# Nine-token partitions, row-tiled attention and two early rounds of three experts in an attention-plus-experts kernel

## The chip, the cores and the metric

One core of one Trainium2 chip. The time is device microseconds (us) of one execution; a shorter time is better. The runs landed on several chips of the kind, and the kernel before does not take the same time on all of them: its medians were 599.9, 585.1, 599.4 and 585.0 us on the four chips of the experiments (called A, B, C and D here). So kernels are compared within one chip, through the kernel before that ran there too. Where times of two chips stand side by side, the text says so.

Engines in the profile: PE is TensorE (PEld its weight loads), DVE VectorE, ACT ScalarE, POOL GpSimd (it issues the cast loads and all gathers and scatters), SP SyncE (it issues the transposing reads).

## The reference

Linear attention with a feature map, whose result is the token matrix x, then a noisy top-2 router and eight experts.

```python
# q, k, v: (8 batches, 8 heads, 576 tokens, 64) float32
phi = lambda x: np.where(x > 0, x, np.exp(x) - 1.0) + 1.0
kv  = einsum('bhsd,bhse->bhde', phi(k), v);  z = phi(k).sum(axis=2)
x   = einsum('bhsd,bhde->bhse', phi(q), kv) / (phi(q).z + 1e-6)   # -> (4608, 512)
noisy = x @ w_gate + log1p(exp(x @ w_noise)) * noise              # (4608, 8)
# ... the two largest per token, softmax of the two -> top2, top2_w
for e in range(8):                       # w1 (512,1024), w2 (1024,512)
    h = maximum(x[mask_e] @ w1[e], 0);  out[mask_e] += top2_w * (h @ w2[e])
```

## The kernel before

It handles the eight batches in four groups of two. For each group: loads (with a cast to bf16), feature map, `kv`, `num`, routing, then a **dispatch**: 18 indirect transfers on POOL that write each token's row twice into `x_sorted`, sorted by expert. When all four groups are dispatched the experts run, 10 tiles of 128 rows each (80 tiles in all): a transposing read `xt`, `mm1` (first layer), `mm2` (second layer, called the tail of a tile), and per tile a **gather** of what the token's first expert wrote to `out` (into a tile `L`) and a **scatter** of the sum (from a tile `y`). A bank is one buffer of PSUM, where the matmul results stand until DVE or ACT takes them.

```python
main = lambda t, b: t[b, :, 0:512, :].rearrange("h (p c) d -> p h (c d)", c=4)   # + 64-token tails
...
for ci in range(NC):                                   # num: 9 blocks of tokens
    for hp in range(4):
        nc.tensor.matmul(out=ps[:, hp, 0:KVW], lhsT=pqs[j][:, hp, ...], rhs=kvbds[j][:, hp, :], ...)
    ...                                                # four DVE operations per block
# ---- (cut) experts
for e in range(E):
    gate, si, gi = self.meta(...)
    for n in (512, 512, 256):
        xt = ...; nc.sync.dma_start(out=xt, in_=self.x_sorted[...], transpose=True)
        hT = self.mm1(w1, xt, n)
        if prev is not None:
            flush(prev)                                # mm2, y, scatter of the block before
        if t0 == 0:
            if e + 3 < E: self.load_w(e + 3)
            for t in range(T_CAP):                     # all gathers of the expert at once
                L[t] = self.gather(gi[:, t : t + 1]) if e > 0 else None
        prev = ...
# pools: weights 3, xt 4, L 12, y 6; PSUM: 4 banks for h, 3 for y
```

A scheduler fixes each engine's order at build time; at run time an engine waits at the head of its list (n3_one below shows it on DVE: 14.75 us behind an operation of 0.17).

Of the kernel before, what the change touches and what calls it, by code (L numbers as in the profile page):

```python
# [15 lines left out]
P = 128  # L16
# [6 lines left out]
NG = 4  # L23
NC = 9
T_CAP = 10
CAP = T_CAP * P
REGION = N_TOK
ROW_W = HD + 16
BIG = 1.0e6
KVW = 162  # L30

# [6 lines left out]
def build_constants(ctx, tc, consts, w_gate, w_noise, noise):  # L38
    nc = tc.nc
    c = {}  # L40

# [19 lines left out]

    c8 = consts.tile([P, E], FP32, name="c8")
    nc.gpsimd.iota(c8[:], pattern=[[-1, E]], base=E, channel_multiplier=0,
                   allow_small_or_imprecise_dtypes=True)
    c["c8"] = c8

    tokid = consts.tile([P, NC], FP32, name="tokid")
    nc.gpsimd.iota(tokid[:, 0:8], pattern=[[S, 2], [1, 4]], base=0, channel_multiplier=4,
                   allow_small_or_imprecise_dtypes=True)
    for half in range(2):  # L70
        nc.gpsimd.iota(tokid[64 * half : 64 * half + 64, 8:9], pattern=[[0, 1]],
                       base=512 + S * half, channel_multiplier=1,
                       allow_small_or_imprecise_dtypes=True)
# [14 lines left out]

    wst = consts.tile([P, 4, 16], FP32, name="wst")
# [11 lines left out]

    noise_sb = consts.tile([P, NG, NC, E], FP32, name="noise_sb")
    for b in range(B):
        g, j = divmod(b, 2)
        nc.scalar.dma_start(
            out=noise_sb[:, g, 4 * j : 4 * j + 4, :],
            in_=noise[b * S : b * S + 512, :].rearrange("(p c) e -> p (c e)", c=4),
        )
    for j in range(2):
        src = noise[512 + j * S : 512 + j * S + 64, :]  # L110
        src = bass.AP(tensor=src.tensor, offset=src.offset,
                      ap=[src.ap[0], [2 * S * E, NG], [1, E]])
        nc.scalar.dma_start(out=noise_sb[64 * j : 64 * j + 64, :, 8, :], in_=src)
# [4 lines left out]
    c["carry"] = carry  # L118
    return c


class PhaseA:
    def __init__(self, ctx, tc, q, k, v, x_sorted, c):
        self.tc, self.nc, self.c = tc, tc.nc, c
        self.q, self.k, self.v, self.x_sorted = q, k, v, x_sorted
        nc = tc.nc
        pool = lambda name, bufs, **kw: ctx.enter_context(tc.tile_pool(name=name, bufs=bufs, **kw))
        self.ld = pool("A_ld", 3)
        self.mx = pool("A_mx", 2)
        self.pers = pool("A_pers", 1)  # L130
        self.tmp = pool("A_tmp", 2)
        self.php = pool("A_php", 2)
        self.kvp = pool("A_kvp", 3)
        self.pq = pool("A_pq", 3)
        self.rt = pool("A_rt", 2)
        self.ps_kv = pool("A_ps_kv", 2, space=PSUM)
        self.ps_t = pool("A_ps_t", 2, space=PSUM)
        self.ps_num = pool("A_ps_num", 2, space=PSUM)
        self.vt = []
        for i in range(4):  # L140
            t = self.pers.tile([P, 12, 256], BF16, name=f"v{i}")
            nc.vector.memset(t[:, 8:12, :], 1.0)
            self.vt.append(t)
        self.vm = []
        for i in range(2):
            t = self.pers.tile([P, 12, D], BF16, name=f"vm{i}")
            nc.vector.memset(t[:, 8:12, :], 1.0)
            self.vm.append(t)
        self.xrow = []
        for i in range(2):  # L150
            t = self.pers.tile([P, NC, ROW_W], BF16, name=f"xrow{i}")
            nc.vector.memset(t[:, :, HD:ROW_W], 0.0)
            self.xrow.append(t)

    def load(self, g):
        nc = self.nc
        st = {"g": g, "k": [], "q": [], "v": []}
        km = self.mx.tile([P, 8, D], BF16, name="km")
        qm = self.mx.tile([P, 8, D], BF16, name="qm")
        vm = self.vm[g % 2]  # L160
        main = lambda t, b: t[b, :, 0:512, :].rearrange("h (p c) d -> p h (c d)", c=4)
        for j in range(2):
            b = 2 * g + j
            kt = self.ld.tile([P, 8, 256], BF16, name="kt")
            qt = self.ld.tile([P, 8, 256], BF16, name="qt")
            vt = self.vt[b % 4]
            nc.gpsimd.dma_start(out=kt[:], in_=main(self.k, b))
            nc.gpsimd.dma_start(out=km[64 * j : 64 * j + 64], in_=self.k[b, :, 512:S, :].rearrange("h p d -> p h d"))
            nc.gpsimd.dma_start(out=vt[:, 0:8, :], in_=main(self.v, b))
            nc.gpsimd.dma_start(out=vm[64 * j : 64 * j + 64, 0:8, :], in_=self.v[b, :, 512:S, :].rearrange("h p d -> p h d"))  # L170
            nc.gpsimd.dma_start(out=qt[:], in_=main(self.q, b))
            nc.gpsimd.dma_start(out=qm[64 * j : 64 * j + 64], in_=self.q[b, :, 512:S, :].rearrange("h p d -> p h d"))
            st["k"].append(kt); st["q"].append(qt); st["v"].append(vt)
        st["km"], st["qm"], st["vm"] = km, qm, vm
        return st

    def phi(self, src, nc_, name):

        nc = self.nc
        n = 512 * nc_  # L180
        flat = src[:].rearrange("p a b -> p (a b)")
        e = self.tmp.tile([P, n], BF16, name=f"e{nc_}")
        t = self.tmp.tile([P, n], BF16, name=f"t{nc_}")
        r = self.php.tile([P, 4, nc_, P], BF16, name=name)
        nc.scalar.activation(out=e[:], in_=flat, func=ACT.Exp)  # L185
        nc.vector.tensor_scalar(out=t[:], in0=flat, scalar1=0.0, scalar2=1.0, op0=ALU.max, op1=ALU.add)
        half = n // 2
        for two in range(2):
            v = lambda x: x[:, half * two : half * two + half].rearrange("p (h c d) -> p h c d", h=4, d=D)
            nc.vector.tensor_tensor(out=r[:, :, :, 64 * two : 64 * two + 64], in0=v(e), in1=v(t), op=ALU.min)  # L190
        return r

    def kv(self, st, j, phk, phkm):
        nc, c = self.nc, self.c
        kvbd = self.kvp.tile([P, 4, KVW], BF16, name="kvbd")
        vt, vm = st["v"][j], st["vm"]
        po = 64 * j
        for half in range(2):
            ps = self.ps_kv.tile([P, 2, 256], FP32, name="kv_ps")
            for i in range(2):  # L200
                hp = 2 * half + i
                for ci in range(4):
                    nc.tensor.matmul(  # L203
                        out=ps[:, i, 0:192],
                        lhsT=phk[:, hp, ci, :],
                        rhs=vt[:, hp::4, 64 * ci : 64 * ci + 64],
                        start=(i == 0 and ci == 0), stop=False, skip_group_check=True,
                    )
                nc.tensor.matmul(
                    out=ps[:, i, 0:192],  # L210
                    lhsT=phkm[po : po + 64, hp, 0, :],
                    rhs=vm[po : po + 64, hp::4, :],
                    start=False, stop=(i == 1), skip_group_check=True,
                )
            nc.vector.tensor_tensor(
                out=kvbd[:, 2 * half : 2 * half + 2, 0:130],
                in0=ps[:, :, 0:130],
                in1=_ap(c["mask"], [[0, 2], [1, 130]]),
                op=ALU.mult,
            )  # L220
        tp = self.ps_t.tile([P, 1024], BF16, name="t_ps")
        for hp in range(4):
            nc.tensor.transpose(tp[:, hp * P : hp * P + P], kvbd[:, hp, 0:128], c["ident"][:])
        kvt = self.kvp.tile([P, 512], BF16, name="kvt")
        nc.scalar.copy(out=kvt[:], in_=tp[:, 0:512])
        wp = self.ps_kv.tile([P, 2, 256], FP32, name="kv_ps")
        wpv = wp[:].rearrange("p a b -> p (a b)")[:, 0:128].rearrange("p (a b) -> p a b", a=4)
        for hp in range(4):
            nc.tensor.matmul(
                out=wpv[:, hp, :], lhsT=kvt[:, hp * P : hp * P + P], rhs=c["wblk"][:, hp, :],  # L230
                start=(hp == 0), stop=(hp == 3), skip_group_check=True,
            )
        nc.vector.tensor_copy(out=kvbd[:, :, 130:162], in_=wpv)
        return kvbd

    def q_t(self, phq):

        nc, c = self.nc, self.c
        pqt = self.pq.tile([P, 4, 512], BF16, name="pqt")
        for half in range(2):  # L240
            tp = self.ps_t.tile([P, 1024], BF16, name="t_ps")
            for i in range(2):
# [8 lines left out]
    def q_tm(self, phqm):  # L251
# [3 lines left out]
        for hp in range(4):  # L255
            nc.tensor.transpose(tp[:, hp * P : hp * P + P], phqm[:, hp, 0, :], c["ident"][:])
# [127 lines left out]
    def run(self):  # L384
        nxt = self.load(0)
        for g in range(NG):
            st = nxt
            if g + 1 < NG:
                nxt = self.load(g + 1)
# [242 lines left out]
```

## Time and profile before

| | before |
|---|---|
| time, median (three fast runs; a fourth came with the result) | 599.88 us (597.19 to 603.38) |
| dispatch of groups 0 to 3 begins | 74.7, 130.3, 174.1, 221.2 us |
| first expert matmul | 251.1 us |
| expert part to the end | 344 us for 80 tiles |
| PE busy in the whole span | 373.5 of 595.4 us |

The waits view has the engine and line that waited, then what for: us in total, times, longest.

```profile
POOL L L461 <- DMA out_dram<-y,si: 60.6, 6, 16.1
...
PE kv_ps L335 <- DVE A L331: 44.2, 4, 16.4
...
PE h_ps L474 <- DMA xt<-x_sorted: 32.3, 1, 32.3
```

Read three waits from them: PE waits 44.2 us for routing (four times, once per group), 32.3 us once between the last routing and the first `xt`, and POOL's gathers wait 60.6 us, six times, at the turns of experts.

### The profile page before, as it was taken

What the parts mean: (1) busy time and instruction counts of PE and PEld (TensorE: products, weight loads), DVE (VectorE), ACT (ScalarE), POOL (GpSimd) and SP (SyncE); (2) the same over time, 40 slices, a digit from 0 to 9 for tenths busy, and PEclk for the clock granted to TensorE, in tenths of its full rate; (3) what the DMA queues carried; (4) which work ended last, traced back from release to release, by engine and by line L of the source; (5) the groups of instructions that cost most, each with busy time, mean ns of one, the idle gap of its engine ahead of it and who ended that gap; (6) DMA issues with size and microseconds to landing.
All of it is one profiled execution on the core that took longest, in us unless ns stands there. A gap on an engine that the chain in (4) does not pass through costs nothing. (4 is left out here: it accounts for less than half of the span.)

```text
span 595.4 us, 5833 instructions
## 1 busy us (share of the span) xinstructions
PE 373.5 (63%) x1976; PEld 194.5 (33%) x1976; DVE 221.8 (37%) x638; ACT 170.2 (29%) x265; POOL 288.7 (48%) x315
## 2 busy tenths in 40 slices
PE   0173173137245300199989928969948968989984
PEld 0151142015124100045444404425424434444442
DVE  4359655375650560413233104314304304333122
ACT  0466444025021120062333401421511321423410
POOL 6445378427427117204346516725706726565364
PEclk9996555556555555589999978998987998998998
DMA  9999954995602002555864993993893995573153
GB/s 168 210 191 191 191 131 101 192 209 157 124 27 102 36 10 106 128 91 130 184 101 121 184 110 80 228 140 101 217 120 101 243 146 145 189 157 145 57 160 128
DMA packets 122985, 82.65 MB, mean 139 GB/s; under 512 B 74164, under 2 KB 108980, under 8 KB 122944
## 3 DMA queue, kind: packets, MB, share of 16 engines
q0 software_dynamic: 65888, 69.02, 56.8%
q1 hardware_dynamic: 54272, 12.98, 14.8%
q10 hardware_dynamic: 2784, 0.18, 0.4%
q8 instruction: 17, 0.28, 0.2%
q14 instruction: 24, 0.20, 0.1%
HBM read 80.72 MB, written 32.87 MB: 191 GB/s over the span
## 5 line engine op out<-in xcount | busy, mean ns | idle before, releaser
L474 PE MATMUL h_ps<-xt,w 128*128 128x512 bf16 (+1 forms) x768 | 150.5, 355 | 39.5 <-DMA xt<-x_sorted 32.3
L476 ACT ACTIVATE hT<-h_ps 128x512 bf16<-128x512 f32 (+1 forms) x192 | 99.4, 527 | 260.8 <-PE h_ps L474 209.2
L483 PE MATMUL y_ps<-w,hT 128*128 128x512 bf16 x640 | 149.8, 392 | 36.5 <-DVE y L489 36.5
L490 POOL DMA_INDIRECT out_dram<-y,si x80 | 79.4, 992 | 97.4 <-DVE y L487 39.9
L474 PEld LDWEIGHTS <-w 128*128 128x128 bf16 x768 | 77.8, 101 | 111.1 <-issue 46.9
L376 POOL DMA_INDIRECT x_sorted<-xrow,posi x72 | 73.6, 1022 | 78.9 <-DVE xrow L373 33.7
L461 POOL DMA_INDIRECT L<-out_dram,gi x70 | 70.6, 1009 | 82.1 <-DMA out_dram<-y,si 60.6
L483 PEld LDWEIGHTS <-hT 128*128 128x128 bf16 x640 | 64.1, 100 | 115.5 <-issue 45.3
L489 DVE SCALAR_TENSOR_TENSOR y<-y_ps,gate,L 128x512 f32<-128x512 f32 x70 | 51.1, 731 | 98.8 <-PE y_ps L483 60.6
L460 DVE MEMSET L<- 128x512 f32 x70 | 34.0, 485 | 34.4 <-DMA x_sorted<-xrow,posi 24.4
L270 PE MATMUL num_ps<-kvbd,pqt 128*128 128x162 bf16 x128 | 22.2, 324 | 38.6 <-DVE lwt L293 34.6
L203 PE MATMUL kv_ps<-v,phk 128*128 128x192 bf16 x128 | 26.0, 360 | 19.0 <-DVE phk L190 19.0
L335 PE MATMUL kv_ps<-A,ut 128*128 128x72 bf16 x4 | 0.9, 219 | 44.2 <-DVE A L331 44.2
L270 PEld LDWEIGHTS <-pqt 128*128 128x128 bf16 x128 | 13.2, 130 | 45.6 <-DVE lwt L293 41.3
L248 ACT COPY pqt<-t_ps 128x1024 bf16<-128x1024 bf16 x16 | 16.0, 1014 | 32.5 <-PE t_ps L244 10.6
L287 DVE TENSOR_TENSOR xrow<-num_ps,rden 128x512 bf16<-128x512 f32 x36 | 24.7, 687 | 0.5
L444 DVE SCALAR_TENSOR_TENSOR isf<-meta 128x10 f32<-128x10 f32 x8 | 1.4, 174 | 58.5 <-DMA meta<-x_sorted 58.5
L203 PEld LDWEIGHTS <-phk 128*128 128x128 bf16 x128 | 14.1, 131 | 23.6 <-DVE phk L190 19.0
L244 PE MATMUL t_ps<-ident,phq 128*128 128x128 bf16 x128 | 16.0, 306 | 8.0 <-ACT pqt L248 4.5
L185 ACT ACTIVATE e<-kt 128x2048 bf16<-128x2048 bf16 x8 | 15.2, 1912 | 10.7 <-DMA kt<-in_k_dram 7.9
L487 DVE TENSOR_SCALAR y<-y_ps,gate 128x512 f32<-128x512 f32 x10 | 7.5, 750 | 28.7 <-PE y_ps L483 28.7
L244 PEld LDWEIGHTS <-phq 128*128 128x128 bf16 x128 | 13.7, 144 | 9.2 <-issue 9.2
(116 smaller groups left out, 277.2 us busy)
## 6 DMA issues: line engine op xcount, KB each, us to landing
w<-in_moe_w_dram POOLq DMA_DIRECT2D x32, 512.0 KB
kt<-in_k_dram POOLq DMA_DIRECT2D x8, 512.0 KB
v<-in_v_dram POOLq DMA_DIRECT2D x8, 512.0 KB
qt<-in_q_dram POOLq DMA_DIRECT2D x8, 512.0 KB
x_sorted<-zrow SPq DMA_DIRECT2D x8, 264.0 KB, 6.6
out_dram<-y,si POOLq DMA_INDIRECT x80
x_sorted<-xrow,posi POOLq DMA_INDIRECT x72
L<-out_dram,gi POOLq DMA_INDIRECT x70
```

What stands on the lines that cost most here:

```text
L203: nc.tensor.matmul(out=ps[:, i, 0:192], lhsT=phk[:, hp, ci, :], rhs=vt[:, hp::4, 64 * ci : 64 * ci + 64], start=(i == 0 and ci == 0), stop ...
L244: nc.tensor.transpose(tp[:, i * 512 + ci * P : i * 512 + ci * P + P], phq[:, 2 * half + i, ci, :], c["ident"][:],)
L270: nc.tensor.matmul(out=ps[:, hp, 0:KVW], lhsT=pqs[j][:, hp, cc * P : cc * P + P], rhs=kvbds[j][:, hp, :], start=(hp % 2 == 0), stop=(hp % ...
L287: nc.vector.tensor_tensor(out=_ap(xrow[:, ci, 0:HD], [[64, 4], [256, 2], [1, 64]]), in0=_ap(ps, [[256, 4], [64, 2], [1, 64]]), in1=_ap(rd, ...
L376: r = nc.gpsimd.indirect_dma_start(out=self.x_sorted, out_offset=bass.IndirectOffsetOnAxis(ap=posi[:, ci, sl : sl + 1], axis=0), in_=xrow[ ...
L460: nc.vector.memset(L[:], 0.0)
L461: nc.gpsimd.indirect_dma_start(out=L[:].bitcast(INT32), out_offset=None, in_=self.out.bitcast(INT32), in_offset=bass.IndirectOffsetOnAxis( ...
L474: nc.tensor.matmul(out=ps[:, 0:n], lhsT=w1[:, dc, fc * P : fc * P + P], rhs=xt[:, dc, 0:n], start=(dc == 0), stop=(dc == 3))
L476: nc.scalar.activation(out=hT[:, fc, 0:n], in_=ps[:, 0:n], func=ACT.Relu)
L483: nc.tensor.matmul(out=ps[:], lhsT=hT[:, fc, t * P : t * P + P], rhs=w2[:, fc, :], start=(fc == 0), stop=(fc == 7))
L489: nc.vector.scalar_tensor_tensor(out=y[:], in0=ps[:], scalar=gate, in1=L[:], op0=ALU.mult, op1=ALU.add)
L490: r = nc.gpsimd.indirect_dma_start(out=self.out, out_offset=bass.IndirectOffsetOnAxis(ap=si, axis=0), in_=y[:], in_offset=None, bounds_che ...
```

## The change

Intent: shorten attention by giving every partition nine neighbouring tokens of two batches (no 64-token tails, half the load transfers) with `kv` and `num` split over halves of the array; and fill PE's idle time in attention with 18 of the 80 expert tiles, in two rounds of experts 0 to 2: 512 rows each after group 1, 256 more after group 2. A row count clamp keeps later groups out of those rows. The late part is rewritten with it.

```diff
+ROUNDS = [(1, 512), (2, 768)]                     # (after group, rows per expert)
-        ... loads: main(b) and 64-token tails, 12 per group
+        in_=getattr(self, t)[2 * g + j].rearrange("h (p c) d -> p h (c d)", c=9)   # 6 per group
...                                                # kv: row halves; num: column halves; DVE work per 3 blocks
+        nc.scalar.activation(out=fld(0)..., in_=c["tokid"], ...)       # token id: DVE -> ACT
...
+    for i, (after, q) in enumerate(ROUNDS):       # clamp: rows below q are closed
+        if after == u: cnt[i] = carry;  carry[:, 0:E1] = max(carry[:, 0:E1], q)
...                                                # expert(): per block of up to 4 tiles
-            hT = self.mm1(w1, xt, n);  flush(prev)
+            mm1 two chunks | tail | mm1 two chunks | tail ...          # tails of the block before between mm1
-            if t0 == 0: gathers of all ten tiles
+            for t in range(t0, t0 + n // P): L[t] = self.gather(...)   # gathers block by block
...                                                # main
+            pa.route(g)
+            for i, (after, _) in enumerate(ROUNDS):
+                if after == g: early(i)                                # experts 0..2 between groups
+    pb.psum_y.append(ps(ctx, "ps_y2", 3, "right"))                     # beside the old pool of 1
+    def rot(self, pools, what): ... return pools[i % len(pools)]       # one of each pool in turn
+    for e in range(E1, 5): pb.load_w(e, 1)                             # two weight sets as the late part begins
```

## The prediction

> **What bounds the kernel now.** I read the page's forty slices first, then the groups by line, then the timeline of POOL, and last the busy time cut into stretches.
>
> ```profile
> PE   0173173137245300199989928969948968989984
> PEclk9996555556555555589999978998987998998998
> DMA  9999954995602002555864993993893995573153
> ...
> L483 PE MATMUL y_ps<-w,hT 128*128 128x512 bf16 x640 | 149.8, 392 | 36.5 <-DVE y L489 36.5
> L376 POOL DMA_INDIRECT x_sorted<-xrow,posi x72 | 73.6, 1022 | 78.9 <-DVE xrow L373 33.7
> L461 POOL DMA_INDIRECT L<-out_dram,gi x70 | 70.6, 1009 | 82.1 <-DMA out_dram<-y,si 60.6
> ```
>
> The slices show two programs one after the other. Up to slice 17 (attention and routing) PE is mostly idle at a granted clock near 0.5; from slice 18 (experts) it is nearly full at 0.9 to 1.0, with dents. The dents are the idle time in the last column: y waits for the gather, the gather (L461) waits 60.6 us for the scatters before it. Cut into stretches:
>
> ```profile
> core 0: us, PE busy (x) PEld busy (x) DVE busy (x) ACT busy (x) POOL busy (x), PEclk, DMA share, GB/s
> 0.00:75.00 75.00, 22.22 (x156) 14.58 (x156) 45.11 (x143) 32.23 (x29) 35.42 (x56) 0.82 1.45 190
> 130.00:174.00 44.00, 20.11 (x145) 12.93 (x144) 26.56 (x89) 12.53 (x14) 20.73 (x20) 0.54 0.50 114
> 174.00:221.00 47.00, 18.38 (x132) 12.05 (x129) 20.32 (x83) 8.82 (x12) 17.43 (x18) 0.50 0.14 52
> 251.00:595.00 344.00, 292.81 (x1408) 141.84 (x1408) 97.04 (x212) 99.41 (x192) 165.84 (x170) 0.92 0.68 143
> ```
>
> The cuts are where each group's dispatch to the sorted rows begins (74.7, 130.3, 174.1, 221.2 us) and the first expert matmul (251). Attention takes 251 us, of which PE is busy 81 and no engine is full after 75: it is a chain. The experts take 344 us. Their matmul work at full clock is 276: the timeline shows 32 matmuls of 512 columns in 6.91 us for four tiles of mm1 and again in 6.91 for four of mm2, so 3.455 us a tile, times 80. The other 68 us are dents at the turn of experts. The timeline of POOL shows one with no weights in flight and one with:
>
> ```profile
> 397.44 1.08 POOL L461 DMA_INDIRECT L<-out_dram,gi  x1 [10.25 <-DMA out_dram<-y,si]
> ...
> 518.89 0.97 POOL L490 DMA_INDIRECT out_dram<-y,si  x1 [0.76 <-DVE gate L441]
> 522.12 1.05 POOL L461 DMA_INDIRECT L<-out_dram,gi  x1 [2.25 <-issue]
> ...
> 533.93 1.00 POOL L461 DMA_INDIRECT L<-out_dram,gi  x1 [0.30 <-issue]
> 537.60 1.02 POOL L490 DMA_INDIRECT out_dram<-y,si  x1 [2.66 <-DMA L<-out_dram,gi]
> ```
>
> Scatter to gather costs 2.25 us and gather to scatter 2.66 when quiet; each transfer holds POOL 1.30 us with its gap. Where weights load, the wait is 6.96, 16.14, 10.25, 14.52 and 10.37 us at the five turns.
>
> **What the Trainium skill says.** (1) "TensorE: Matmul & The Clock Gate", Part 1 (the HAM clock gate): the array runs at half clock until about 3.4 us of sustained work. The trace agrees: from 251.1 the weight loads come every 0.43 us, and at about 257 the pace doubles; 5.5 us at half rate. (2) "DMA: Bandwidth & Descriptors", Anatomy of one DMA, SWDGE path: about 2.0 us fixed for a transfer, mostly until the write is confirmed. The 2.25 and 2.66 us agree. (3) The same page, Specifications: at least 512 B for line rate. In the first 75 us 13752 of 36469 packets are under 512 B, yet the sixteen engines are full at 190 GB/s counted at the bf16 destination, which is about twice that read in float32; so I give the longer pieces no gain in rate. (4) "TensorEngine Tiling (Array Packing)", Instruction Overhead: a very short matmul costs as much as one of 60 columns. Here eight half-width matmuls (L277) take 0.75 us and four full ones (L270) 0.72, so pairs on the two halves do overlap.
>
> **The change part by part.**
>
> Loads. A group (two batches) is 3.54 MB at the destination: 18.5 us at 191 GB/s, four groups 74. The total is unchanged; 48 load transfers become 24, and the 128 B tails go. What changes is order: group 3's v now sits on POOL behind the 18 dispatches of group 0 (74.7 to 99.6); in the new text each load comes ahead of the dispatch of its turn. Zero rows (2.2 MB) and six noise transfers leave the start; ACT, held until 14.46 us by fourteen issues, is free earlier. Group 0 should dispatch at about 62 instead of 75.
>
> Attention matmuls. kv goes from 40 to 72 per group, two row halves at a time; num from 40 to 144 short ones on column halves. At the cold rate I put PE at 24 us a group, against 18 to 20 now; it isn't the bound, and early expert work may warm it.
>
> DVE of num. Per group now 9 x (0.158 + 0.196 + 0.687 + 0.281) = 11.9 us. New: 9 x 0.69 + 3 x about (0.17 + 0.21 + 0.55) = 9.0. Route drops two small ops and adds five for the levels. Two table loads of 1.28 us per group go away through one preloaded table; and the token-id write that sat in DVE's queue waiting for an earlier dispatch (4.84 us at 156.4, 5.26 at 101.4) moves to ACT. Sum: about 3 + 2.6 + 5, some 10 us of a 45 us period: 35 us.
>
> Early rounds. With the given inputs expert counts after two groups are 544, 612, 583 for experts 0 to 2 and after three 840, 897, 854, so 512 and 768 rows are full: 3 x 6 = 18 of 80 tiles, 62.2 us of PE, leave the expert phase. Their dispatches must have landed: group 1's ends about 62 + 35 + 23 = 120, so round one starts near 125. It costs 12 x 3.455 = 41.5, plus 2.7 for the cold clock, plus two gather turns with only one y bank (I take 5 each): 54 us, to about 179. Engines run in order, and the static order decides whether groups 2 and 3 run beside it. If they do, group 3's dispatch (18 x 1.27 = 23 us, behind 26 us of gathers and scatters on POOL) ends near 200. If they queue behind it: dispatches at about 200 and 235, end near 260. I take 230 for the first late expert matmul, against 251.
>
> Late experts. 62 tiles x 3.455 = 214 us of PE. But gathers are now issued per block of four tiles, and each waits for the scatters of the block before; a scatter in turn waits for all gathers before it. Loop for four tiles: gathers 3 x 1.30 + 1.0 = 4.9, landing 2.7, scatters 4.9, landing 2.3: 14.8 us against 13.8 of PE. For two tiles: 2.3 + 2.7 + 2.3 + 2.3 = 9.6 against 6.9. So a whole expert takes 39.2, and the late part 3 x 14.8 + 5 x 39.2 = 240. Five weight sets are still loaded there; each now costs its turn (mean of the five waits 11.6 minus 2.3) 9.3 us: 47. Sum 287, plus 1 for a slightly longer last block: 288, against 344.
>
> Total: 230 + 288 = 518.
>
> **The rivals.** (a) PE becomes the bound: groups overlap round one and the late part hides its loop. Weights for experts 3 and 4 are far ahead, mm2 tiles are interleaved with mm1, which gives each gather about 8.6 us of other matmuls to hide in. Then 200 + 214 + 45 (half the turns and contention): about 470. (b) In-order blocking: attention of groups 2 and 3 queues behind round one on PE, DVE and ACT, or an early scatter waits in POOL's queue ahead of a dispatch. For it: today PE waits 16.4 us for routing's A with kv ready behind it, and DVE's queue head blocks. Then 265 + 300 = 565. (c) The transfers eat it: 76 gathers instead of 70, 14 of them early, collide with loads, and the finer gather turns, 18 late instead of 7, each pay for weights in the queue. Then 240 + 320 = 560. (d) The gain of the attention rewrite is hidden anyway, since group 1's dispatch and not DVE gates round one: 10 us less gain, 530.
>
> **Range and chances.** The end of attention is uncertain by about 30 us and the late part by about 25; combined some 40. Range 478 to 562. For no gain over 2% (588) both (b) and (c) must come true in full: I give faster 0.90, same 0.07, slower 0.03.
>
> **What would show it.** The first late matmul (row 768 of expert 0) at 230; round one as a stretch of nearly full PE from about 125, at clock 1.0 after 5 us; POOL's dispatch of group 1 ending near 120; a whole late expert every 39 us plus about 9 where weights load; scatter-gather waits on POOL of 2.3 us quiet. The page should show PE busy near 380 us in a shorter span, no table loads after the first, and 228 indirect POOL transfers (222 now). Wrong if dispatches come at a period still near 45, if the stretch between 125 and 230 has PE idle in pieces over 10 us, or if late turns number 18 with waits over 8.

## More of the kernel before

The group line has busy us, mean ns of one, and idle us before it with what ended the idle time.

```profile
L474 PE MATMUL h_ps<-xt,w 128*128 128x512 bf16 (+1 forms) x768 | 150.5, 355 | 39.5 <-DMA xt<-x_sorted 32.3
```

## The result, and the profile after

The changed kernel is slower: median 638.59 us (635.20 to 647.84, 4 runs) against 600.27 us for before, ratio 1.062 with 95% interval 1.053 to 1.071. Ratios here and below are the mean time of one kernel's fast runs over the mean of the other's in the same rounds, so not quite the ratio of the medians quoted. The prediction, 518 us, is wrong in direction.

The profiled execution (span 646.1 us) was 1.1% longer than the next slowest and counts as slow; its structure is that of the experiments' fast profiles (the same kernel with one moved ACT write, run e3_tok below, has span 640.1; its dispatches and its first late matmul begin within 2 us of those here, and its late part takes 316 us instead of 320).

The page after: PE's busy tenths and granted clock in forty slices, then three group lines.

```profile
PE   0454625605984279600056927697979979979740
...
PEclk9875655756997669755586959697998989979985
...
L458 PE MATMUL y_ps<-w,hT 128*128 128x512 bf16 x640 | 171.6, 417 | 73.5 <-DVE y L464 65.5
L450 PE MATMUL h_ps<-xt,w 128*128 128x512 bf16 (+1 forms) x768 | 159.4, 354 | 76.4 <-DMA xt<-x_sorted 75.9
...
L438 POOL DMA_INDIRECT L<-out_dram,gi x76 | 77.6, 1021 | 111.0 <-DMA out_dram<-y,si 77.0
```

Slices 10 to 17, counted from 1, show early expert work (round one is 153 to 236 us), and slices 18 to 20 are empty again: PE now has its long hole after attention later than before (it ends at 325.6 us instead of 251.1), and the late part is a comb of 9s and 7s where before it was 9s and 8s with a few dents. `h_ps` waits 75.9 us for `xt` instead of 32.3; `y_ps` waits 65.5 us for DVE instead of 36.5. Cut into stretches (length, then busy us of each engine, granted clock, DMA share, GB/s):

```profile
core 0: us, PE busy (x) PEld busy (x) DVE busy (x) ACT busy (x) POOL busy (x), PEclk, DMA share, GB/s
...
153.00:233.00 80.00, 54.58 (x296) 26.21 (x296) 14.15 (x48) 20.07 (x34) 36.36 (x37) 0.80 0.28 90
...
273.00:325.60 52.60, 0.89 (x11) 0.48 (x10) 12.03 (x51) 0.94 (x4) 26.29 (x29) 0.50 0.48 103
325.60:646.00 320.40, 234.47 (x1072) 109.02 (x1071) 76.00 (x154) 77.39 (x144) 131.90 (x134) 0.87 0.56 124
```

No engine is full in the first stretch, PE is dead in the second, and the late part takes 320.4 us for 62 tiles, whose work at full pace is 214. The timeline of all engines (start, length, engine, line, and in brackets the idle time before it and its releaser) shows how the attention of groups 2 and 3 got late:

```profile
154.53 0.22 DVE L305 TENSOR_TENSOR A<-oh 128x72 bf16<-128x72 f32 x1
...
190.20 0.20 PE L309 MATMUL misc<-A,ut 128*128 128x72 bf16 x1
...
194.94 0.97 POOL L358 DMA_INDIRECT x_sorted<-xr,posi  x1 [0.91 <-DVE xr L339]
...
285.26 0.95 POOL L358 DMA_INDIRECT x_sorted<-xr,posi  x1 [9.86 <-issue]
...
310.00 1.52 POOL L400 DMA_DIRECT2D w<-in_moe_w_dram  x2 [2.29 <-issue]
...
314.45 18.50 SPq L496 DMA_TRANSPOSE xt<-x_sorted  x1
...
325.63 8.68 PE L450 MATMUL h_ps<-xt,w 128*128 128x512 bf16 x32 [44.60 <-DMA xt<-x_sorted]
```

Group 2's routing has its input A at 154.53, but the ten small matmuls that rank it (L309 to L312) stand in PE's list behind two blocks and more of round one and run at 190.20. Group 2's dispatch begins at 194.94; without rounds it begins at 155.56 (e1_norounds below). Group 3 loses more behind round two: its dispatch begins at 285.26 (before: 221.2). At 310 the late part begins, and so do eight weight transfers; one transpose takes 18.50 us, and the first late matmul is at 325.63. The waits view of after:

```profile
POOL L L438 <- DMA out_dram<-y,si: 77.0, 18, 13.3
PE h_ps L450 <- DMA xt<-x_sorted: 75.9, 3, 44.6
...
ACT xr L340 <- DMA x_sorted<-xr,posi: 31.5, 2, 20.8
...
DVE noisy L288 <- ACT sp L287: 13.6, 2, 13.0
```

The gathers' wait comes 18 times now instead of six. And the token-id write did move to ACT, but there it blocks in the same way: 20.8 us at the head of ACT's list, for which DVE waits 13.0 us with group 2's softplus.

### The profile page after: what moved, and what is told of

The parts are those of the page before. It is cut to its first block, busy times and chain, and to the rows that moved or that the text cites. A ratio compares the mean times of both kernels' runs of the same rounds, so it can differ in the third digit from the quotient of the medians.

```text
span 646.1 us, 6747 instructions
## 1 busy us (share of the span) xinstructions
PE 380.0 (59%) x2520; PEld 202.9 (31%) x2520; DVE 204.6 (32%) x495; ACT 169.3 (26%) x271; POOL 274.5 (42%) x295
## 5 line engine op out<-in xcount | busy, mean ns | idle before, releaser
L458 PE MATMUL y_ps<-w,hT 128*128 128x512 bf16 x640 | 171.6, 417 | 73.5 <-DVE y L464 65.5
L450 PE MATMUL h_ps<-xt,w 128*128 128x512 bf16 (+1 forms) x768 | 159.4, 354 | 76.4 <-DMA xt<-x_sorted 75.9
L358 POOL DMA_INDIRECT x_sorted<-xr,posi x72 | 75.4, 1048 | 58.1 <-issue 27.2
L173 ACT ACTIVATE e<-kq 128x2304 bf16<-128x2304 bf16 x16 | 33.5, 2125 | 27.7 <-PE misc L191 17.3
L191 PE MATMUL misc<-v,e 64*128 64x192 bf16 x288 | 24.9, 325 | 21.9 <-DVE e L177 20.0
L240 PE MATMUL num<-kvbd,pqt 128*64 128x128 bf16 x288 | 18.8, 267 | 25.8 <-DVE xr L259 22.8
L240 PEld LDWEIGHTS <-pqt 128*64 128x64 bf16 x576 | 20.6, 136 | 34.5 <-DVE xr L259 21.3
L191 PEld LDWEIGHTS <-e 64*128 64x128 bf16 x288 | 20.8, 122 | 25.8 <-DVE e L177 20.0
L259 DVE TENSOR_TENSOR xr<-num,rden 128x512 bf16<-128x512 f32 x36 | 23.5, 685 | 1.8 <-PE num L240 1.0
L177 DVE TENSOR_TENSOR e<-e,kq 128x2304 bf16<-128x2304 bf16 x16 | 21.3, 1342 | 0.1
L225 ACT COPY pqt<-misc 128x1024 bf16<-128x1024 bf16 (+1 forms) x20 | 17.9, 932 | 12.6 <-PE misc L224 12.6
L400 POOL DMA_DIRECT2D w<-in_moe_w_dram x16 | 11.9, 745 | 12.1 <-DMA w<-in_moe_w_dram 8.9
L403 POOL DMA_DIRECT2D w<-in_moe_w_dram x16 | 12.4, 776 | 8.4 <-DMA kq<-in_k_dram 8.4
```

The source lines that it names most:

```text
L173: nc.scalar.activation(out=ev(two), in_=xv(two), func=ACT.Exp)
L191: nc.tensor.matmul(out=ps[j][:, i, 0:192], lhsT=phk[half, hp, ci, :], rhs=vt[half, hp::4, 64 * ci : 64 * ci + 64], start=(i == 0 and ci == ...
L240: nc.tensor.matmul(out=out[half], lhsT=pqt[ci][:, hp, half], rhs=kvbd[:, j, hp, cols], start=start, stop=stop, skip_group_check=True)
L259: nc.vector.tensor_tensor(out=_ap(xr[:, ci, 0:HD], [[64, 4], [256, 2], [1, 64]]), in0=_ap(ps, [[128, 4], [64, 2], [1, 64]]), in1=_ap(rden[ ...
L358: r = nc.gpsimd.indirect_dma_start(out=self.x_sorted, out_offset=bass.IndirectOffsetOnAxis(ap=posi[:, ci - c0, sl : sl + 1], axis=0), in_= ...
L450: nc.tensor.matmul(out=ps[:, 0:n], lhsT=w1[:, dc, fc * P : fc * P + P], rhs=xt[:, dc, 0:n], start=(dc == 0), stop=(dc == 3))
```

## The experiments

Theory after reading the two traces: the early rounds do not run beside attention, they push it back, because every engine takes its list in order (T1). Rivals: the new attention is itself slow (R1); the new late part is the loss (R2), by its 18 gather turns, by its weight burst, or by its buffers' turn-taking; the token-id write on ACT is what holds group 2 (R3). All 17 runs below gave correct results. The changed kernel itself was not run again beside them: 638.6 us and a first late matmul at 325.6 are of the result's chip, where before took 600.3, about as on A and C.

| run | chip | median, us | ratio to before (95%) | first late matmul, us | from there to the end, tiles |
|---|---|---|---|---|---|
| e1_norounds | A | 632.0 | 1.066 (1.053 to 1.078) | 244.1 | 385, 80 |
| e2_priog | A | 638.9 | 1.078 (1.067 to 1.090) | (rounds overlap it) | |
| e5_ge | A | 618.5 | 1.042 (1.026 to 1.058) | 322.0 | 295, 62 |
| e3_tok | A | 640.1 | 1.079 (1.067 to 1.090) | 324.2 | 316, 62 |
| n1_attn | B | 566.6 | none: one fast run, 555.9 | 219.6 | 345, 80 |
| f1_rot | B | 641.3 | 1.095 (1.087 to 1.103) | 321.1 | 321, 62 |
| f2_stg | B | 636.9 | 1.089 (1.083 to 1.095) | 310.3 | 323, 62 |
| f4_all | B | 578.9 | 0.980 (0.972 to 0.987) | 307.8 | 264, 62 |
| a_ge_rot | C | 587.7 | 0.987 (0.977 to 0.997) | 317.2 | 262, 62 |
| a_ge_stg | C | 604.4 | 1.013 (1.004 to 1.022) | 313.2 | 290, 62 |
| p1_prio | C | 595.5 | 0.995 (0.978 to 1.013) | (rounds overlap it) | |
| r1_laterp | C | 610.5 | 1.023 (1.014 to 1.033) | 304.6 | 304, 68 |
| r1_later | D | 571.0 | none: two fast runs, 565.8 and 566.4 | 276.5 | 288, 68 |
| n2_best | D | 539.1 | 0.924 (0.915 to 0.933) | 205.6 | 332, 80 |
| n3_one | D | 549.3 | none: one fast run, 530.5 | | |
| n2_again | C | 574.5 | 0.964 (0.957 to 0.970) | 232.8 | 335, 80 |
| n4_dve | C | 560.1 | 0.937 (0.927 to 0.946) | | |

The last two columns are of the profiled run. The medians are over all runs, the ratios over the fast ones. Runs more than 1.5% above a kernel's fastest count as slow here, also where their clocks are alike: f4_all (two of four runs) and n4_dve (two of six) keep two fast runs each. On A only three of the seven runs of before count as fast (590.4 to 597.5), so the ratios of A are some 1% higher than against its median.

### The rounds taken out: e1_norounds

```diff
-ROUNDS = [(1, 512), (2, 768)]
+ROUNDS = []
```

> The list of early rounds is emptied: the new attention and the new late part stay, all 80 tiles run late. My theory: the new attention is as quick as I predicted, and it is the early rounds that push the dispatches of groups 2 and 3 back. Then the first late expert matmul comes at 215 to 235 us instead of 325, the late part takes 360 to 380 (80 tiles at 3.455 us, plus about 4 us at each of 24 block turns, plus the weights), and the total is 580 to 610, below the 636 with the rounds. Rival one: the new attention itself is slow (short matmuls on halves of the array, loads and zero rows ahead of the dispatches); then attention still ends past 260 and the total is 640 or more. Rival two: the late part is the loss; then the total is over 620 although attention ends near 225.

Total 632.0 us, hardly less than with rounds: my theory's total was missed, and the second rival's hit (over 620 although attention ends near 225). The parts show that both are at work. The last transfer of the last dispatch, on the same chip without rounds (e1_norounds) and with them (e5_ge, whose edit touches only what comes later):

```profile
224.93 0.96 POOL L358 DMA_INDIRECT x_sorted<-xr,posi  x1 [0.30 <-issue]
```

```profile
303.88 0.96 POOL L358 DMA_INDIRECT x_sorted<-xr,posi  x1 [0.30 <-issue]
```

The rounds cost attention **79 us**, for 62 us of PE work. That much of T1 holds. But the first matmul comes 19 us after that transfer, where in the kernel before it took 8 (18 transfers from 221.2 at 1.27 us put the last at 242.8), and the late part takes 385 us where before took 344. So R2 holds too, and is the larger part: against the profile of before (of another chip, on which before is as fast as on A), attention gives 18 us, the start takes 11 more and the late part 41 more. The rounds add little to that in the end: with them (e3_tok, chip A) the last transfer comes 81 us later and the late part is 69 us shorter. The timeline of this run at the start of the late part:

```profile
228.17 1.51 POOL L400 DMA_DIRECT2D w<-in_moe_w_dram  x2 [2.28 <-issue]
...
228.14 21.07 SPq L496 DMA_TRANSPOSE xt<-x_sorted  x2
...
244.11 9.79 PE L450 MATMUL h_ps<-xt,w 128*128 128x512 bf16 x32 [43.02 <-DMA xt<-x_sorted]
```

The weights of experts 3 and 4 go out in the same microsecond as the first two transposes (SPq is SP's queue), which occupy that queue for 21.07 us together; 16 us pass from the first issue to the first matmul. The Trainium skill, "DMA: Bandwidth & Descriptors", Issuing engines are not separate DMA queues, says that transfers of all issuing engines run on the same 16 DMA engines and interleave; the trace agrees, with this number, and f2_stg below moves the weights away.

### The attention alone: n1_attn

The rounds are out and the expert phase is put back to that of before.

```diff
+ROUNDS = []
+            self.mm1(w1, xt, hT, n, range(0, 8))          # then all tails
+            if t0 == 0: load_w(e + 3); gathers of all tiles of the expert
+    # xt 4, L 12, y 6, three y banks; no weight loads at the start of the late part
```

> The attention rewrite alone: no early rounds, and the expert phase put back to that of the kernel before (gathers of a whole expert at its first block, all mm1 of a block ahead of the tails of the block before, three weight buffers refilled one expert at a time, four xt buffers, three y banks, twelve L, six y). The run without rounds but with the new expert phase took 385 us from its first expert matmul at 244. If the new expert phase is the larger loss, this run has its first expert matmul at 235 to 248 and an expert part of 340 to 350, total 580 to 595, faster than before by 1 to 3%. Rival: the row order of the nine-token partitions or something in the attention spoils the expert part (different scatter rows, other DMA packets); then the expert part stays at 370 or more and the total over 610.

The expert part is 344.7 us, within half a microsecond that of before (344.3), and the first expert matmul comes at 219.60 instead of 251.1. (The 251.1 is of another chip, where before is 15 us slower.) The total is 555.9 in its fast run and 566.2 to 570.3 in the others, against 585.1: 2.5 to 5% faster, more than expected, and each run is below the fastest of before on its chip (581.6). R1 falls. The profile is of a run of 566.2. Its stretches after group 3's routing, same columns as above:

```profile
189.80:219.60 29.80, 0.00 (x1) 0.00 (x0) 0.69 (x6) 0.00 (x0) 17.26 (x18) 0.50 0.39 113
219.60:564.00 344.40, 291.86 (x1408) 142.01 (x1407) 91.72 (x178) 101.00 (x192) 165.34 (x170) 0.91 0.66 143
```

There is a stretch of 29.8 us in which PE does nothing at all: the last dispatch and the first transposes. I come back to it.

### The token id and the priority: e3_tok, e2_priog, p1_prio

```diff
+        with tc.issue_after(ln.ins):                  # e3_tok: behind this routing's softplus
             nc.scalar.activation(out=fld(0)..., in_=c["tokid"], ...)
+            with tc.high_priority(): pa.group(g)      # e2_priog
+            with tc.high_priority(): pa.route(g)
```

> The token-id write on ACT is queued behind the softplus of the same group's routing, so that it no longer stands at the head of ACT's queue waiting for the dispatch two groups before (10.8 and 20.8 us). If this block is what delays group 2, its dispatch moves from 195 to about 175 and the total falls by 15 to 20 us to 616 to 622. My theory: group 2's routing matmuls stand behind the rounds on PE anyway, so the ACT wait goes away and the total stays at 628 to 640.

> The text is unchanged but attention and routing of every group are given priority over the early rounds when the static order of each engine is made. The ten small matmuls of group 2's routing then stand ahead of the rounds' work on PE instead of 35 us behind it, and group 2's dispatch stands earlier on POOL. My theory: group 2's dispatch starts near 160 instead of 195, group 3's near 225 to 240 instead of 285, the first late expert matmul comes at 270 to 290 instead of 325, and the total is 590 to 605. Rival: the engines are simply shared and the same work takes the same time in any order; then the first late matmul stays within 10 us of 325 and the total at 630 to 640.

> All three late mends, with attention and routing given priority over the early rounds and the token-id write behind its own routing's softplus. On the unmended late part the priority brought the first late matmul from 325 to 303 us and the total not at all. If the late part had swallowed that gain, it shows now: first late matmul at 285 to 295 instead of 308, ratio to before 0.95 to 0.965. Rival: an expert block begun earlier only ends its rounds no earlier, since early work cut short moves behind the attention; then the ratio stays at 0.975 to 0.985.

e3_tok: no gain, 640.1 us; the first late matmul stayed at 324.2. R3 falls. e2_priog: the last transfer of group 3's dispatch began 17 us earlier (289.6 against 306.8), group 2's dispatch began later instead of earlier (214.5 against 194.9), and the total did not move. p1_prio is e2_priog with e3_tok's edit and the mended late part of below; it came out at 0.995, no better than the mended kernel without priority on another chip (0.980). What the timeline of p1_prio shows: the gathers of round two, two per expert, begin at 294, 307 and 318 us, behind the last dispatch, and the late part's first gathers at 329. Early work that is no longer ahead of attention is behind it. But the priority did more than the text of the edit says: it also moved the q loads behind the dispatches on POOL (the third group's is issued at 90.6 in e2_priog, behind group 0's dispatch, and at 45.5 in after), and group 2's dispatch is at 214.5 in both runs. The two effects are not separated, so these runs neither show nor exclude that priority alone would help.

### The late part: e5_ge, f1_rot, f2_stg, f4_all, a_ge_rot, a_ge_stg

Three suspects, one edit each, then all three, then two pairs.

```diff
+        if t0 == 0: LL = {t: self.gather(...) for t in range(nt)}      # ge: an expert's gathers at once, L in one pool of 12
+    pb.psum_y = [pb.psum_y[0]] + [pb.psum_y[1]] * 3                    # rot: each bank in its turn
+    pb.yp = [pb.yp[0]] * 2 + [pb.yp[1]] * 5
-    for e in range(E1, 5): pb.load_w(e, 1)                             # stg: one weight set at a time,
+        with tc.issue_after(pb.lastg): pb.load_w(e + 3, 1)             #      behind expert e's gathers
```

> In the late part the gathers of a whole expert (ten, or four for experts 0 to 2) are issued at its first block, as in the kernel before, instead of block by block; nothing else changes. If the finer gather turns cost what I think (about 4 us of PE idle at most of the 18 block turns), five turns of two per whole expert go away and the late part shortens by 15 to 35 us: total 605 to 622. Rival: the interleaved tails hide the fine turns, and ten gathers in a row only make a longer hold on POOL at the turn; then the total is 636 or up to 650. The first late matmul stays at 325 in both.

> The changed kernel in full, only the turn-taking of the late buffers is mended: it took one buffer of a small pool and one of a large pool in turn, so one y bank of four was due again after two tiles; now each of the four y banks, eight L and seven y buffers is used in its turn. If the 4 us of PE idle at each late block turn is the wait for that one y bank, PE's 65 us of waiting for DVE's y falls by 30 or more, and the total falls by 15 to 30 us to 607 to 622. Rival: the turn is set by scatter, gather and landing on POOL's queue, and deeper banks only let PE run two tiles further before the same wait; then under 8 us, 628 to 638.

> The changed kernel in full, only the late weight loads are moved: instead of two experts' weights at the very start of the late part and three more soon after, expert e's late gathers come first and then the weights of expert e+3, one set at a time. If the burst is what held the first late transposes (one of 18.5 us where 5.7 is usual) and gave the gather waits of 12 to 13 us, the first late matmul comes at 312 to 318 instead of 325 and three PE gaps of 10 to 14 us shrink to about 5: total 610 to 622. Rival: the same bytes cost the same wherever they stand, and expert 3 then waits for its weights; total 630 to 645.

> The changed kernel with its early rounds, and three mends of the late part together: gathers of a whole expert at once, y banks and y buffers used each in its turn, weights one set at a time behind the gathers. If the late part's loss lies in these, the late part goes from about 313 us to 265 to 280 (62 tiles at 3.455 us are 214) and the total to 585 to 600, the level of the kernel before, although the first late matmul is still at 315 to 325. Rival: the parts overlap and only the best of them counts: 612 to 620, as with the gathers alone.

> The changed kernel with two of the three late mends: gathers of a whole expert at once, and y banks and y buffers each in its turn; the weight burst at the start of the late part stays. Gathers alone gave a ratio to before of 1.042, all three 0.980; banks alone and weights alone gave nothing. If the banks are what whole-expert gathers still needed (one y bank of four due again after two tiles), this run lies within 0.015 of all three, 0.98 to 1.00. Rival: it is the weight loads, which with ten gathers behind them hold up the turn; then this run stays at 1.025 to 1.045.

> The changed kernel with the other pair: gathers of a whole expert at once, and weights one set at a time behind the gathers; the turn-taking of the y banks stays as it was. If the banks carry the gain, this run stays at a ratio to before of 1.02 to 1.04; if the weights carry it, 0.98 to 1.00; if each carries a part, both pairs lie near 1.01.

Three expectations were missed (f1_rot and f2_stg gained nothing; f4_all gained more than it should); e5_ge and a_ge_rot came out as expected. Whole-expert gathers alone bring the late part from 316 to 295 us (both on A). The banks alone and the weights alone leave it at 321 and 323 us (both on B). Part of f2_stg's expectation did come true: its first late matmul is at 310.3 us against 321.1 in f1_rot, 7.8 us behind the last transfer instead of 18.3, so the burst of weights did hold the start; the late part gave the gain back. Yet gathers and banks together give 262 (C), and adding the weights gives 264 (B) with a start some 9 us earlier. On C, gathers and weights without the banks give 290. So the parts neither add up nor overlap: **they come one behind the other**, the gathers first, then the banks. The reading that fits: with gathers block by block, POOL's loop sets the pace: four gathers, their landing, four scatters, their landing; a y bank more only lets PE run further ahead to the same wait. The waits of f1_rot (banks mended, gathers by block) and of f4_all:

```profile
POOL L L438 <- DMA out_dram<-y,si: 68.1, 18, 10.4
PE y_ps L458 <- DVE y L464: 64.3, 16, 8.7
```

```profile
POOL L L438 <- DMA out_dram<-y,si: 38.0, 7, 11.0
PE y_ps L458 <- DVE y L464: 32.1, 9, 8.3
```

PE's wait for `y` is as long in f1_rot as in the changed kernel (65.5 us); with seven turns in place of 18, and all three mends, it halves. The gathers alone bring it to 54.4 (e5_ge). That it then hangs on the banks, the two pairs on C show, a_ge_rot first, a_ge_stg second:

```profile
L458 PE MATMUL y_ps<-w,hT 128*128 128x512 bf16 x640 | 156.8, 389 | 31.1 <-DVE y L464 20.6
```

```profile
L458 PE MATMUL y_ps<-w,hT 128*128 128x512 bf16 x640 | 167.4, 409 | 70.5 <-DVE y L464 70.5
```

In the stretch of the changed kernel behind its weight loads, first gathers of experts 3 to 7 come at 421.6, 465.5, 507.7, 548.6 and 591.7 us: 42.5 us an expert. In f4_all those of experts 4 to 7 come at 428.7, 466.4, 496.4 and 531.1: 34.1 us, about PE's own pace (10 tiles of 3.455); from expert 3 (383.5), with weights loading beside it, to expert 4 it is 45.3.

### Where the early work is queued: r1_laterp, r1_later

On the mended late part: one round of 512 rows, traced and queued on PE behind group 2's routing, so that the routing cannot come late.

```diff
+ROUNDS = [(1, 512)]
-                if after == g: early(i)
+                if after + 1 == g:
+                    with tc.issue_after(pa.rk_last):   # the last ranking matmul of group 2
+                        early(i)
```

> All three late mends, one early round instead of two (512 rows of three experts), and it is queued on PE behind group 2's routing, with priority for attention: it may run only beside group 3. With no rounds PE sat idle for 53 us between 150 us and the first expert matmul at 220. If early experts can be had in idle time at all, the first late matmul comes at 230 to 245 and 68 tiles remain at 4.25 us: 290; total 520 to 545, ratio 0.89 to 0.93, better than attention alone (0.968). Rival: on in-order engines the 12 tiles still push group 3's dispatch back by most of their 41 us of PE and 26 us of POOL; then the first late matmul is at 265 or later and the ratio 0.96 to 1.0, no better than no round.

> As r1_laterp but without the priority for attention, which had moved the loads of q behind the dispatches and delayed group 2 by 30 us on its own. Group 2's dispatch should start near 160 again. One round of 12 tiles stands on PE between group 2's routing and group 3's attention. If a round between groups is serial wherever it stands, group 3's dispatch starts 40 to 55 us later than the 190 it had without rounds, the first late matmul comes at 260 to 275, and with 68 late tiles at 4.25 us (289) the total is 550 to 565, ratio 0.93 to 0.965, no better than no round. If it fits into idle time, first late matmul at 230 to 245 and ratio 0.88 to 0.92.

r1_laterp missed both its expectations, and it mixes two causes: the priority it also had moved the q loads behind the dispatches, and group 2's dispatch began at 190.7. r1_later has no priority; its timeline:

```profile
246.98 0.96 POOL L359 DMA_INDIRECT x_sorted<-xr,posi  x1 [20.28 <-DVE ovi L542]
...
276.47 0.58 PE L454 MATMUL h_ps<-xt,w 128*128 128x512 bf16 x1 [31.85 <-DMA xt<-x_sorted]
```

The last transfer of group 2's dispatch began at 179.8, as it should, but group 3's began at 246.98 and the first late matmul came at 276.5. Without rounds it was at 205.6 on the same chip (n2_best below): **71 us for 12 tiles**, which are 41.5 us of PE work. Its two fast runs, 565.8 and 566.4 us, stand against 537.5 to 543.4 with no round; it was serial, as expected, and a little worse. In both places in which a round between groups was tried, it costs more than it gives.

### No rounds and the mended late part: n2_best, n2_again

> No early rounds, and the changed kernel's late part with the three mends (gathers of a whole expert, banks in turn, weights one set at a time) and the token-id write behind its softplus. First expert matmul at 215 to 222 as in the run with the old expert phase; 80 tiles at 4.25 us are 340: total 550 to 565, ratio 0.95 to 0.97. If interleaving tails with mm1 is worth something over the old phase, the expert part is under 340; if not, it is 340 to 350.

> The control again: no early rounds, mended late part. 535 to 545 us, ratio to before 0.92 to 0.93, as before.

```diff
+ROUNDS = []                                            # with ge, rot, stg and the token id of e3_tok
```

539.1 us, ratio 0.924, better than expected. The first expert matmul is at 205.63 and the 80 tiles take 332 us: the interleaved tails with whole-expert gathers are worth 13 us over the old phase's 345 (measured on another chip). From the page and the timeline of n2_best:

```profile
L459 PE MATMUL y_ps<-w,hT 128*128 128x512 bf16 x627 | 151.8, 384 | 0.5
...
205.63 0.58 PE L451 MATMUL h_ps<-xt,w 128*128 128x512 bf16 x1 [31.71 <-DMA xt<-x_sorted]
```

PE's wait for `y` is gone (0.5 us). On chip C the same kernel gave only 0.964, a missed expectation: 27 of the 30 us between the two profiles lie in front of the experts (first matmul at 232.8), in one wait that I cannot explain:

```profile
174.12 0.76 DVE L197 TENSOR_TENSOR kvbd<-misc,mask 128x260 bf16<-128x260 f32 x2 [28.15 <-remote]
```

The trace names no releaser that it knows ("remote"). It is there in both profiles of that chip with this order (28.15 and, in n4_dve, 30.4 us) and absent on D. The traces of A and C, and those of before and after, hold fewer semaphore events than those of B and D (4666 in n2_again, 6730 in n2_best, the same kernel), so "remote" may only mean that the releasing event is missing, and releasers are less sure in those traces. This stays open.

### Early work in the dead stretch: n3_one, n4_dve

Only expert 0's first 768 rows (6 tiles, no gathers; the buffer pools are cut to fit), queued on PE behind group 3's ranking matmuls and on POOL behind group 3's dispatch.

```diff
+E1 = 1;  ROUNDS = [(2, 768)]
+                    with tc.issue_after(pa.last):
+                        with tc.issue_after(pa.rk_last), tc.issue_after(pa.dve_last):   # dve_last: n4_dve only
+                            early(i)
```

> As n2_best, but 768 rows of expert 0 alone (6 tiles, 20.7 us of PE, no gather) may run once groups 0 to 2 are dispatched, queued on PE behind group 3's routing and on POOL behind group 3's dispatch: in the 30 us in which PE had nothing to do. If early work pays only in truly idle time, group 3's dispatch stays near 190, the row-768 matmul of expert 0 starts at 215 to 225 as before, and the total is 15 to 22 us under n2_best: ratio 0.92 to 0.94. Rival: its transposes and scatters collide with the dispatch and the gain is under 8 us.

> As n3_one, but the early rows' work stands behind group 3's routing on DVE as well as on PE and POOL. If the 14.75 us that DVE stood at the head of its queue was what the early work cost, group 3's dispatch starts at 175 to 178 as in the control instead of 190, and the six tiles come off the late part: 8 to 20 us under the control, 520 to 532, ratio 0.89 to 0.915. Rival: the late part of expert 0 gains nothing since its transposes wait for group 3's dispatch in any case and the six tiles' scatters stand in front of the later ones; then within 5 us of the control.

n3_one was unclear (530.5, 547.0, 551.7, 551.9 us). Its timeline shows the first of these catching on DVE:

```profile
173.84 0.17 DVE L426 SCALAR_TENSOR_TENSOR gate<-meta 128x6 f32<-128x6 f32 x1 [14.75 <-DMA meta<-x_sorted]
...
175.57 2.06 PE L241 MATMUL num<-kvbd,pqt 128*64 128x128 bf16 x24 [15.87 <-DVE xr L260]
```

The early rows' gate, a 0.17 us operation, stood at the head of DVE's list waiting 14.75 us for a read that follows group 2's dispatch, and behind it stood group 3's evictions (the DVE operations that take matmul results out of PSUM), and behind those PE. n4_dve queues it behind group 3's routing on DVE as well. Against its control on the same chip and in the same rounds (n2_again) it is 0.937 to 0.964, or 14 us in the medians, and its slowest run (564.8) is below the control's fastest (569.3): inside the expected 8 to 20 us, though the absolute numbers of the expectation (520 to 532) were those of chip D. Group 3's dispatch begins at 205.6 in it and at 203.2 in the control, so the early work no longer holds it (in n3_one it began at 190.8 against 176.3 in n2_best, both on D); its early matmuls run from 203 us, while the control's first matmul is at 232.8. This is the only early expert work that paid, and n4_dve and n2_best both beat the kernel before. It differs from r1_later not only in place but in size (6 tiles against 12) and in having no gathers; no run separates these.

## Why the prediction was wrong, point by point

- **"Group 0 should dispatch at about 62"**: 65.55. Near. The zero rows, now written during attention, stood in front of it: n1_attn's dispatch (66.64) waited for them.
- **"35 us" a group**: per-operation costs were right (DVE's `num` work: 9 x 0.685 + 3 x (0.548 + 0.179 + 0.295) = 9.2 us against 9.0), the period was not: in n1_attn (chip B) dispatches begin at 66.6, 115.9, 159.9 and 189.8, a mean of 41. The first gap is 49: the loads of one group and two weight sets stand on POOL between the two dispatches, and the first eight transfers of group 1 came 2.6 us apart instead of 1.27. Attention alone still ended at 219.6, before the 230 that I gave with rounds.
- **"24 us a group"** for attention's matmuls: PE was busy 18.1, 13.4 and 14.4 us between the dispatches of n1_attn. That a very short matmul costs as much as one of 60 columns, which was cited there, no run isolates.
- **"moves to ACT. Sum: about 3 + 2.6 + 5"**: the 5 us of the token id were no saving; the wait moved along and grew to 10.8 and 20.8 us. It cost nothing only because group 2 was late anyway (e3_tok).
- **"54 us, to about 179"** for round one: it began at 153.4, ran to about 236, and so took 83. It began late because group 1's dispatch ended near 147, not 120. PE was busy 54.6 of the 80 us to 233, group 3's `kv` included; the rest was waiting, most of it (8.0 and 11.3 us) for `y`, whose gathers stood on POOL between the transfers of group 2's dispatch (205.1 to 214.2).
- **"I take 230 for the first late expert matmul, against 251." This is the step that failed**: 325.6. I weighed rounds beside attention (200) against rounds in front of it (260) and took the middle. The runs show neither: 18 tiles of 62 us pushed the last dispatch back by 79 us (e1_norounds against e5_ge), 12 tiles of 41.5 us by 71 (r1_later against n2_best). So what was wrong is the overlap: I let the early tiles run half beside attention, and they delayed it by more than their own work. I had seen rival (b), engines blocked in order, and sized it at 265; that rival was the mechanism, and its size was 60 us short.
- **"288" for the late part**: 316 (e3_tok) and 320 (after). Mis-sized terms: a whole expert takes 42.5 us where I had 39.2, so 17 us for five; the other 11 to 15 lie in the experts before, where the weights load, and at the end. My loop of 14.8 us for four tiles took gather and scatter turns as hidden behind PE up to 1 us; with block-by-block gathers the turn was the pace. The 47 us for five weight sets ("each now costs its turn") were not the error: in f4_all, which loads the same weights one set at a time, PE has four gaps over 1 us behind its first late matmul, 23.8 us together, the last ending at 421.5; four of the five sets load before that. So about half of the 47 remains there.
- **Rival (c)**, finer gather turns, was right in kind and in size: 18 waits instead of six, 77.0 us instead of 60.6, and a late part of 316 to 320 us where (c) had 320. I had asked for both (b) and (c) "in full" for no gain, and gave slower 3%. Both came, (b) beyond full. All three of the prediction's signs of being wrong appeared: dispatch periods of 50, 79 and 90 us (45 was the limit), PE idle 20.5 and 11.3 us in one piece between 125 and 230, and 18 late turns, two of them over 8 us (12.6 and 13.4).
- **Sums.** The case "beside" does not come out as written: 62 + 3 x 35 + 23 is 190, with 26 us of POOL work in front 216, not 200. Rival (a) sums to 459, not 470. Neither touches the outcome.
- **The clock.** The Trainium skill, "TensorE: Matmul & The Clock Gate", Part 1 (half rate until sustained work), was cited for a cost of 2.7 us at the start of round one. That came out: its first 40 matmuls took 11.0 us, where 40 at the full pace of 6.91 us for 32 take 8.6. What was left out: in the trace after, the granted clock is 0.80 over round one and 0.87 over the late part (0.87 in e3_tok's fast profile too) against 0.92 over the experts before. The 640 `y_ps` matmuls are busy 171.6 us after and 149.8 before. How much of that is the clock and how much is operands that came late, no run separates.

**What stays open**: the 28 us wait on chip C, and with it how much of the front's length on any one chip is the kernel's own; and the two clusters of n1_attn, n3_one, r1_later, f4_all and n4_dve.

## What to carry to other kernels

Work pulled into another phase's idle time must be queued behind that phase on every engine it touches, not only on the one that was idle: a 0.17 us operation waiting for data, or ten tiny matmuls standing behind a block, hold up the chain that sets the end. Idle PE time inside a dependency chain is not free room; the stretch in which nothing of the chain is left to issue is (here that paid for one piece of six tiles, n4_dve). And when a loop through several queues paces a phase, mend the outermost limit first: the mends behind it measure as nothing until then, so a single-edit experiment that shows no gain does not clear its suspect.

## What the Trainium skill lacked or had wrong

- "DMA: Bandwidth & Descriptors", Issuing engines are not separate DMA queues: right, but the page has no time for a transposing read beside other transfers. Two transposing reads beside eight weight transfers of 512 KB held SP's queue for 21.07 us (e1_norounds) and one for 18.50 (after); three took 6.43 with no weights beside them (n1_attn).
- No page that I read tells what an engine's list in order costs when its head waits for a transfer: 14.75 us on DVE (n3_one), 20.8 us on ACT (after), and 35.7 us for which group 2's routing stood ready behind expert matmuls on PE (A at 154.53, its matmul at 190.20, after).
- "DMA: Bandwidth & Descriptors", Anatomy of one DMA gives the fixed time of one software transfer but not its rate behind loads: the first eight transfers of a dispatch came 2.6 us apart behind queued loads and weights, the later ones 1.27 (n1_attn).
- "TensorE: Matmul & The Clock Gate", Part 1: it fits, though the half rate lasted 5.5 us from 251.1 in the trace before, where the page has about 3.4. The granted clock of 0.50 in the dead stretches, 0.80 in a round of broken work and 0.91 to 0.93 in steady experts (n1_attn, n2_best) are numbers for it.
- No page explains the wait of 28.15 us that came in both profiles on one chip and not on another for the same kernel, nor medians of 585 and 599 us of one kernel on different chips.
